# Two chunks of a gated feed-forward in seven-product form on 64x64 tiles

## The chip, the cores and the metric

The kernel runs on one core of a Trainium2 chip. The metric is the device time of one execution in microseconds, lower is better. TensorE (PE) does the matrix products, VectorE (DVE), ScalarE (ACT) and GpSimd (POOL) work on tiles, and SyncE (SP) issues most of the transfers. A tile in SBUF or PSUM has 128 rows (partitions); matrix products write to PSUM, which has eight banks of 512 float32 a row.

## The reference

An attention block (a sketch of degree two, four batches, four heads, 1088 positions, 32 per head) gives 4352 tokens of 128 features. They go through a gated feed-forward of width 1536, all in float32:

```python
gate = 1.0 / (1.0 + np.exp(-(x @ w_gate)))   # x: 4352 x 128, w_gate: 128 x 1536
val = x @ w_val                              # w_val: 128 x 1536
return (gate * val @ w_out).astype(np.float32)   # w_out: 1536 x 128
```

The change touches the feed-forward alone.

## The kernel before

The tokens are kept transposed, in `xT`, 128 features by 4352 tokens. They are cut into nine chunks: 0 to 7 of 512 tokens and a last one of 256. The width of 1536 is cut into twelve blocks j of 128. The unit of the loop is a wave (`w1`): for one j of one chunk PE makes gate and value, each 128x512, by four products of 128 rows, 64 columns and 512 tokens (L556), into two banks of a buffer `wave` that exists twice. Such a product gives two matmul records in the trace. ACT then makes the sigmoid `sg` from the gate half (L564), and DVE multiplies it with the value half into `g` (L599, L592 for the last chunk). One wave later the buffer's turn comes again, so the mult of wave n must be over before wave n+2 starts.

For chunks 1 to 7 the product with w_out is done by pairs of j. The two 64-column halves and the two 256-token halves of a pair make a 2x2 block product, and it is done in seven products in place of eight (L381, in `w2_a` and `w2_b`). POOL makes the four differences of tokens that it needs (`token_sums`, L371); the sums of weights, `ws`, are made once at the start. The results gather in two PSUM banks, `acc0` and `acc1`. At the end of a chunk ACT copies halves across (L487, L522, L529), DVE adds (L496) and transposes (L533), and SP issues the stores (L393): four where the chunk lies in one batch, eight where it lies in two (chunk 6 does, chunk 7 does not). The last chunk has six waves of two j each, and its w_out products have the tokens in the columns of the array (`w2_end`, L451).

The order of every engine's work is the order in which the program states it. Function `slot` runs one wave after the other: the mult of the wave before, the w_out products that are due, then the new wave. The attention work of batches 1 to 3 is put between the waves by hand, in `plan`. Waves are counted through: wave 0 is the first of chunk 0, waves 24 to 35 belong to chunk 2, wave 71 is the last of chunk 5, and chunks 6 and 7 are waves 72 to 95. The tokens of batch 3, from token 3264 on, are written to `xT` by DVE from 197.22 us on; chunk 6 begins at token 3072.

Of the kernel before, what the change touches and what calls it, by code (L numbers as in the profile page):

```python
# [8 lines left out]
F32 = mybir.dt.float32  # L9
# [3 lines left out]
ALU = mybir.AluOpType  # L13
ACTF = mybir.ActivationFunctionType
MUL = ALU.mult

P = 128


@with_exitstack  # L20
def kernel(
# [12 lines left out]
    nc = tc.nc  # L34
# [3 lines left out]
    F = R * R  # L38
# [3 lines left out]
    assert DM == H * D == P and D == 32 and R == 8 and S % 32 == 0 and NTOK % 512 == 256  # L42

    T = S // 32

    NJK = 9
    KBASE = [0, 9, 17, 25]
# [5 lines left out]
    ld = ctx.enter_context(tc.tile_pool(name="ld", bufs=1))  # L53
    sbA = ctx.enter_context(tc.tile_pool(name="sbA", bufs=2))
    raw = ctx.enter_context(tc.tile_pool(name="raw", bufs=NJ // 2))
    sbN = ctx.enter_context(tc.tile_pool(name="sbN", bufs=1))
    sbG = ctx.enter_context(tc.tile_pool(name="sbG", bufs=3))

    dram = ctx.enter_context(tc.tile_pool(name="dram", bufs=1, space=bass.MemoryType.DRAM))

    psm = ctx.enter_context(tc.tile_pool(name="psm", bufs=2, space=bass.MemoryType.PSUM))
    pso = ctx.enter_context(tc.tile_pool(name="pso", bufs=1, space=bass.MemoryType.PSUM))
    ps2 = ctx.enter_context(tc.tile_pool(name="ps2", bufs=1, space=bass.MemoryType.PSUM))

    ctx.enter_context(tc.manual_schedule(
            engines={
# [62 lines left out]
    class Short:  # L129
# [31 lines left out]
        def total(self):  # L161
            nc.gpsimd.tensor_tensor(  # L162
                out=self.head, in0=self.head, in1=self.tail.bitcast(I32), op=ALU.add
            )
# [183 lines left out]

    xT = const.tile([P, NTOK], F32, tag="xT")

    moe = {"sum": -1, "ci": 0, "w": 0, "n": 0, "ready": 0, "acc": None, "gate": None, "todo": [], "late": [], "copies": []}

    def fast(ci):
        return 0 < ci < len(tok_chk) - 1 and tok_chk[ci][1] == TCH

    def weight_sums(n0, n1):
        w = w_sb[:, 2].rearrange("p (n f) d -> p f n d", f=2)[:, :, n0:n1]
# [22 lines left out]
    def product(out, lhsT, rhs, start, stop):  # L380
        nc.tensor.matmul(  # L381
            out=out, lhsT=lhsT, rhs=rhs, start=start, stop=stop, skip_group_check=True
        )
# [18 lines left out]

    def store_end(acc):
        b, r = divmod(tok_chk[-1][0], S)
        o_sb = [sbA.tile([P, P], F32, tag="o_sb", name="o_end") for _ in range(2)]
        for u, copy in enumerate((nc.scalar.copy, nc.vector.tensor_copy)):
            copy(out=o_sb[u], in_=acc[u])
        for u, eng in enumerate((nc.scalar, nc.sync)):
            eng.dma_start(
                out=bass.AP(  # L410
                    tensor=out.tensor,
                    offset=out.offset + (b * S + r // 32 + u) * DM,
                    ap=[[T * DM, 32], [2 * DM, 4], [1, DM]],
                ),
                in_=o_sb[u],
            )

    def w2(ci, j0, jn, g):
# [13 lines left out]
        if j0 + jn == NJ:  # L432
# [2 lines left out]
            moe["store"] = lambda: store(  # L435
                ci, lambda g4: o_sb[32 * g4 : 32 * g4 + 32], nc.scalar
            )

    def w2_end(ci, j0, jn, g):
        if j0 == 0:  # L440
            moe["sum"] = ci
            moe["acc"] = [
                pso.tile([P, TCH], F32, tag="acc0", name="moeout0")[:, :DM],
                ps2.tile([P, 2, TCH], F32, tag="two", name="moeout1")[:, 0, :DM],
            ]
        acc = moe["acc"]
        for u in range(2):
            for jj in range(jn):
                j = j0 + jj
                for c in (u * P, u * P + 64):  # L450
                    nc.tensor.matmul(  # L451
                        out=acc[u][c % P : c % P + 64],
                        lhsT=g[:, jj, c : c + 64],
                        rhs=w_sb[:, 2, j, :],
                        start=(j == 0),
                        stop=(j == NJ - 1),
                    )
        if j0 + jn == NJ:
            store_end(acc)


    fst = {}

# [31 lines left out]
    def add(out, in0, in1):  # L495
        nc.vector.tensor_tensor(out=out, in0=in0, in1=in1, op=ALU.add)  # L496
# [44 lines left out]
    def w1():  # L541

        ci = moe["ci"]
        t0, tw = tok_chk[ci]
        jn = TCH // tw
        j0 = moe["w"] * jn
        wv = psm.tile([P, 2, TCH], F32, tag="wave", name="wave")

        tp = tw // 2 if ci == 0 and j0 == 0 else tw
        turn = (moe["w"] // 2) % 2  # L550
        for o in range(0, tw, tp):
            for which in range(2):
                for jj in range(jn):
                    for c in (0,) if ci == 0 else (1 - turn, turn):
                        d = slice(0, P) if ci == 0 else slice(64 * c, 64 * c + 64)
                        nc.tensor.matmul(  # L556
                            out=wv[d, which, jj * tw + o : jj * tw + o + tp],
                            lhsT=w_sb[:, which, j0 + jj, d],
                            rhs=xT[:, t0 + o : t0 + o + tp],
                            start=True,  # L560
                            stop=True,
                        )
        sg = sbG.tile([P, TCH], F32, tag="sg", name="sg")
        nc.scalar.activation(out=sg, in_=wv[:, 0], func=ACTF.Sigmoid)  # L564
        if ci == 0:
            if j0 == 0:
                step("final", 2)
                step("sign", 3, bank="acc1")
            if j0 == 1:
                step("final", 3)  # L570
            if 1 < j0 < NJ - 1:
                narrow_w(j0 + 1, 3)
            if j0 > 0:
                narrow_w(j0 + 2, 1)
                narrow_w(j0 + 2, 2)
            if j0 < 3:
                narrow_w(j0 + 3, 0)
            if j0 > 1:
                narrow_w(j0 + 4, 0)
            if j0 == NJ - 3:  # L580
                weight_sums(0, NJ // 4)
            if j0 == NJ - 1:
                weight_sums(NJ // 4, NJ // 2)
        if moe["w"] % 2 == 0:
            moe["g"] = sbG.tile([P, 2, TCH], F32, tag="g", name="g")
        pair, odd, n = moe["g"], moe["w"] % 2, moe["n"]

        def glu():
            g = pair[:, odd]
            todo = moe["todo"]  # L590
            if jn == 2:
                nc.vector.tensor_tensor(  # L592
                    out=g.rearrange("p (j u s y) -> p j y u s", j=2, u=2, y=4),
                    in0=wv[:, 1].rearrange("p (j y u s) -> p j y u s", j=2, u=2, y=4),
                    in1=sg.rearrange("p (j y u s) -> p j y u s", j=2, u=2, y=4),
                    op=MUL,
                )
            else:
                nc.vector.tensor_tensor(out=g, in0=wv[:, 1], in1=sg, op=MUL)  # L599
            if not fast(ci):  # L600
                lag = 4 if ci else 2
                part = (ci, j0, jn, g.rearrange("p (j t) -> p j t", j=jn))
                todo.append((n + lag, lambda: (w2_end if ci else w2)(*part)))
                return
            if not odd:
                moe["t"] = raw.tile([P, 4, HALF], F32, tag="w_in", name="tsum")
            token_sums(pair, moe["t"], odd)
            if odd:
                part = (ci, j0 // 2, pair, moe["t"])
                todo.append((n + 3, lambda: w2_a(*part)))  # L610
                todo.append((n + 4, lambda: w2_b(*part)))

        moe["gate"] = glu
        moe["w"] += 1
        moe["n"] += 1
        if j0 + jn == NJ:
            moe["ci"] += 1
            moe["w"] = 0

    def glu():  # L620
        if moe["gate"] is not None:
            moe["gate"]()
            moe["gate"] = None

    def slot(group, waves, behind=None):

        if group is not None:
            group()
        todo = moe["todo"]
        for _ in range(waves):  # L630
            more = moe["ci"] < len(tok_chk)
            if more and sum(tok_chk[moe["ci"]]) > moe["ready"]:
                break
            glu()
            for _ in range(2 if moe["ci"] >= len(tok_chk) - 1 else 1):
                if moe["late"]:
                    moe["late"].pop(0)()
            while todo and todo[0][0] <= moe["n"]:
                todo.pop(0)[1]()
            if behind is not None:  # L640
                behind()
                behind = None
            if more:
                w1()
            for copy in moe["copies"]:
                copy()
            moe["copies"] = []
            if more:
                continue
            if not todo:  # L650
                break
            else:
                todo.pop(0)[1]()

    kT_of, qT_of = {}, {}

# [688 lines left out]
    slot(None, 1)  # L1345
    slot(lambda: parts(1), 1)
    moe["store"]()

    def until(n):
        slot(None, n - moe["n"])  # L1350
# [3 lines left out]
    for b in range(2, B):  # L1354
# [24 lines left out]
        load_kq(b + 1)  # L1379
        until(next(at))  # L1380
        slot(lambda: parts(b), 1)
    slot(None, 10**3)


# [28 lines left out]
```

## Time and profile before

| | |
|---|---|
| median of 3 runs | 289.92 us (289.42 to 290.87) |
| span of the profiled execution | 288.1 us |
| what the median has beyond that span | 1.8 us |
| PE busy | 282.6 us, 98% of the span |
| DVE busy | 170.5 us, 59% |
| POOL busy | 160.0 us, 56% |
| ACT busy | 106.6 us, 37% |
| gate/value products of all waves (L556) | 820 records, 201.4 us |
| sigmoid (L564) | 102 x 597 ns |
| mult (L599) | 96 x 688 ns |
| differences of tokens on POOL (L371) | 168, 0.79 to 0.82 us each |
| last PE record ends | about 284.9 us |

In the profile's lines a group is named by its line, its engine and its operation, then the tile written, `<-`, the tiles read, the shape and the count; what follows is the start and the length in us, or for a group the busy time and the mean. "128*64 128x512" is a product with weights of 128 rows and 64 columns and a moving tile of 128 x 512. PEld is the loading of weights, SPq and ACTq are the transfers that SP and ACT issue. In a list of windows each engine has its busy time and its number of instructions, and then follow the granted clock of PE (1.00 is all of it), the busy share of the transfer engines and their GB/s. Ends of PE records are modelled, and the records of neighbouring products overlap, so that a step is best read from start to start.

### The profile page before, as it was taken

To read this page: it belongs to the slowest core of one execution; us is meant where nothing else is said; L and a number is where in the kernel's file an instruction comes from. 1 tells how busy PE (TensorE), PEld (TensorE's weight loads), DVE (VectorE), ACT (ScalarE), POOL (GpSimd) and SP (SyncE) were. 2 spreads that over 40 slices of the span, in tenths; PEclk is the share of its full clock that TensorE was granted. 3 is DMA by queue.
4 is the path that set the end of the run, shared out by engine and by line. 5 is a ranking of instruction groups with operands and counts; after the bars stand their busy time and mean duration, and the time that the engine had idled before them with its cause. 6 is when DMAs were issued, how large, how long until landed. Compare 5 with 4: busy or idle time off the path is not lost.

```text
span 288.1 us, 5783 instructions
## 1 busy us (share of the span) xinstructions
PE 282.6 (98%) x2260; PEld 135.1 (47%) x2260; DVE 170.5 (59%) x292; ACT 106.6 (37%) x215; POOL 160.0 (56%) x222
## 2 busy tenths in 40 slices
PE   8899999999999999999999999999999999999995
PEld 4454433354444444535444445444444444444685
DVE  6977788945748547668446485767245223522571
ACT  3688833222334322523244222532243224421341
POOL 2666682667466387383565496483564646555200
PEclk9999999999999999999999999999999999999999
DMA  7995441766500385352000683020001000020012
GB/s 220 348 360 124 104 156 43 171 150 157 164 3 2 77 198 166 92 161 32 1 0 12 162 158 123 2 30 9 0 3 23 14 2 0 4 35 1 0 19 40
DMA packets 28891, 24.24 MB, mean 84 GB/s; under 512 B 18560, under 2 KB 24064, under 8 KB 28864
## 3 DMA queue, kind: packets, MB, share of 16 engines
q1 hardware_dynamic: 25888, 22.10, 30.1%
q10 hardware_dynamic: 2976, 1.77, 2.1%
q8 instruction: 18, 0.29, 0.4%
q14 instruction: 9, 0.07, 0.1%
HBM read 20.60 MB, written 3.26 MB: 83 GB/s over the span
## 4 chain that ended last, share of the span: by engine, by line
PE 97%; ACT 1%; POOL 0%; DVE 0%; issue 0%
PE wave L556 61%; PE prod L381 22%; PE moeout L425 4%; PE moeout L451 2%; PE warm L301 2%; PE kvz L912 1%; PE nps L1270 1%; PE kps L693 1%; PE kvz L899 1%; PE cqps L839 1%; PE nps L1102 0%; PE denj L1041 0%; PE nps L1054 0%; PE dps L1083 0%; ACT asb L810 0%; POOL gh L727 0%
## 5 line engine op out<-in xcount | busy, mean ns | idle before, releaser
L556 PE MATMUL wave<-xT,w_sb 128*64 128x512 f32 (+3 forms) x820 | 201.4, 565 | 0.1
L564 ACT ACTIVATE sg<-wave 128x512 f32<-128x512 f32 x102 | 60.9, 597 | 158.3 <-PE wave L556 152.3
L599 DVE TENSOR_TENSOR g<-wave,sg 128x512 f32<-128x512 f32 x96 | 66.1, 688 | 87.9 <-ACT sg L564 86.3
L371 POOL TENSOR_TENSOR tsum<-g,tsum 128x256 f32<-128x256 f32 x84 | 68.6, 817 | 71.0 <-DVE g L599 70.9
L556 PEld LDWEIGHTS wave<-xT,w_sb 128*64 128x64 f32 (+1 forms) x820 | 71.0, 140 | 72.7 <-issue 53.0
L371 POOL TENSOR_TENSOR tsum<-g 128x256 f32<-128x256 f32 x84 | 66.6, 793 | 22.1 <-DVE g L599 21.5
L381 PE MATMUL prod<-tsum,ws 128*64 128x256 f32 x252 | 68.4, 380 | 0.0
L381 PE MATMUL prod<-g,w_sb 128*64 128x256 f32 (+1 forms) x170 | 50.3, 378 | 0.0
L381 PEld LDWEIGHTS prod<-tsum,ws 128*64 128x64 f32 x252 | 34.0, 137 | 13.1 <-issue 9.7
L381 PEld LDWEIGHTS prod<-g,w_sb 128*64 128x64 f32 x170 | 23.0, 137 | 30.1 <-issue 25.8
L381 PE MATMUL prod<-tsum,w_sb 128*64 128x256 f32 x84 | 25.0, 380 | 0.0
L381 PE MATMUL prod<-g,ws 128*64 128x256 f32 x84 | 25.0, 379 | 0.0
L162 POOL TENSOR_TENSOR head<-head,tail 128x384 int32<-128x384 int32 (+1 forms) x13 | 13.2, 1023 | 4.4 <-DVE head L157 4.4
L381 PEld LDWEIGHTS prod<-g,ws 128*64 128x64 f32 x84 | 11.5, 137 | 5.7
L425 PE MATMUL moeout<-g,w_sb 128*128 128x512 f32 (+1 forms) x26 | 12.4, 596 | 0.0
L381 PEld LDWEIGHTS prod<-tsum,w_sb 128*64 128x64 f32 x84 | 11.3, 137 | 1.3 <-issue 1.0
L592 DVE TENSOR_TENSOR g<-wave,sg 128x512 f32<-128x512 f32 x6 | 6.8, 1134 | 6.3 <-ACT sg L564 4.7
L772 DVE TENSOR_TENSOR kp<-kab 128x1152 f32<-128x1152 f32 (+1 forms) x8 | 10.2, 1289 | 0.0
L892 DVE TENSOR_TENSOR qp<-qp,bq 128x1152 f32<-128x1152 f32 (+1 forms) x7 | 10.1, 1444 | 0.0
L496 DVE TENSOR_TENSOR res<-prod,other 128x256 f32<-128x256 f32 x14 | 5.9, 425 | 6.3 <-ACT other L487 4.8
L141 POOL TENSOR_SCALAR head<-cap 128x384 f32<-128x384 f32 (+1 forms) x13 | 6.2, 483 | 4.6 <-ACT cap L140 4.6
L152 ACT ACTIVATE tail<-w_in,two__157 128x384 f32<-128x384 uint32 (+1 forms) x12 | 7.3, 618 | 0.0
(130 smaller groups left out, 197.5 us busy)
## 6 DMA issues: line engine op xcount, KB each, us to landing
qp<-dq SPq DMA_DIRECT2D x7, 576.0 KB
bq<-dq SPq DMA_DIRECT2D x14, 288.0 KB
kq<-in_k_dram SPq DMA_DIRECT2D x3, 544.0 KB
kq<-in_q_dram SPq DMA_DIRECT2D x3, 544.0 KB
w_in<-in_moe_w_out_dram SPq DMA_DIRECT2D x6, 256.0 KB
w_in<-in_moe_w_gate_dram SPq DMA_DIRECT2D x5, 256.0 KB
w_in<-in_moe_w_val_dram SPq DMA_DIRECT2D x5, 256.0 KB
v<-in_v_dram SPq DMA_DIRECT2D x8, 144.0 KB
```

Source lines behind the costliest of these rows:

```text
L141: nc.gpsimd.tensor_scalar(out=self.head.bitcast(F32), in0=self.cap, scalar1=122880.0, scalar2=2.0**-15, op0=ALU.min, op1=ALU.max,)
L152: nc.scalar.activation(out=self.tail, in_=self.lo, func=ACTF.Identity, bias=two, scale=2.0**-51)
L162: nc.gpsimd.tensor_tensor(out=self.head, in0=self.head, in1=self.tail.bitcast(I32), op=ALU.add)
L371: nc.gpsimd.tensor_tensor(out=t[:, u], in0=in0, in1=in1, op=ALU.subtract)
L381: nc.tensor.matmul(out=out, lhsT=lhsT, rhs=rhs, start=start, stop=stop, skip_group_check=True)
L425: nc.tensor.matmul(out=moe["acc"][d], lhsT=w_sb[:, 2, j, d], rhs=g[:, jj], start=(j == 0), stop=(j == NJ - 1),)
L556: nc.tensor.matmul(out=wv[d, which, jj * tw + o : jj * tw + o + tp], lhsT=w_sb[:, which, j0 + jj, d], rhs=xT[:, t0 + o : t0 + o + tp], sta ...
L564: nc.scalar.activation(out=sg, in_=wv[:, 0], func=ACTF.Sigmoid)
L592: nc.vector.tensor_tensor(out=g.rearrange("p (j u s y) -> p j y u s", j=2, u=2, y=4), in0=wv[:, 1].rearrange("p (j y u s) -> p j y u s", j ...
L599: nc.vector.tensor_tensor(out=g, in0=wv[:, 1], in1=sg, op=MUL)
L772: eng.tensor_tensor(out=KP[b][:, pi, j0:j1].rearrange("p j m (i l) -> p (j m) i l", i=R), in0=bass.AP(tensor=a0.tensor, offset=a0.offset, ...
L892: nc.vector.tensor_tensor(out=q0, in0=q0, in1=half(BQ[b], n), op=MUL)
```

## The change

Chunks 6 and 7 get their gate and value in another form, in a section of its own at the end of the program. The 2x2 block product here is that of the upper and the lower 64 features with the gate and the value weights of a block, on one side, and with the two token halves, on the other. Seven products (P1 to P7) replace eight. Each is on one half of the rows: 64 features, 256 tokens, and, for one j, two halves of 64 columns. For a pair of j this makes 14 items (the second j is marked by a prime, `P1'`), each of two products of 64x64x256. Items on the lower and the upper half of the rows are listed in turns, and they write to different banks.

The whole section is written out item by item in a string, `ORDER`, that gives each engine its sequence. The letter says what the item is and the number after the colon the pair (0 to 5 are chunk 6, 6 to 11 chunk 7, -2 and -1 the last two pairs of chunk 5, whose w_out is held back into the section):

- P: a gate/value product on half the rows. P1 and P2 go into bank GA, P5 and P3 into GC, P6, P7 and P4 into V; each bank exists twice, so that six banks take the place of the two `wave` buffers and of the bank pair `two`.
- Aa, Ac, Sa, Sc on ACT: copy GA to V, copy GC to SBUF, and the two sigmoids, once GA and GC are complete.
- D1, D2 on DVE: V plus the copy, into GC and into SBUF; M1, M2: the two halves of the mult. Q0 to Q3 on POOL: the differences of tokens for w_out.
- W: two w_out products, on the lower (WL), the upper (WU) or all rows (WF), A or B naming the accumulator.
- E, F: a chunk's end. ACT copies an accumulator to SBUF, SP copies halves across the rows (two transfers for A, three for B), DVE adds (F0 to F5), and F6 transposes and starts the stores on SP.
- C, Y, Z, O: the last chunk's gate/value products, sigmoid, mult and w_out products, now listed between the ends of chunks 6 and 7. T: a sum of tokens of `xT` on POOL.

The seven products need sums of the gate and value weights. For these ACT issues seven transfers (64 rows x 3 x 256 columns, across the halves). They are listed for waves 21 to 24, but stated only once wave 23 is, so that six stand in a row behind wave 23's sigmoid and one behind wave 24's. DVE makes ten sums, one each behind a mult from wave 24 to wave 61, two of 128x768 and eight of 64x768. They need also four differences of tokens of each chunk on POOL, of which chunk 6's are put among the last four waves of chunk 5, and copies of the tokens across the rows, issued by SP.

```diff
+ORDER = """
+P5:1 P1:0 T0:1 P1':1 WLA:-2.1 P1:1 P1':0 P5':1 P5':0 Aa:0 WUB:-2.0 P5:0 WLA:-2.0 Aa:1 P6':0 P2':0
+P6:0 Ac:0 P6':1 P2:1 Ac:1 P6:1 D1:0 P2':1 P2:0 D1:1 Sa:1 P7':0 P3':0 P7:0 P3:0 Sa:0 P3':1 P7':1 D2:0
+Sc:0 WUB:-1.0 WLA:-1.0 P3:1 WLA:-1.1 M2:0 WUB:-1.1 P7:1 Sc:1 P4':0 P5':2 Q0:0 D2:1 P4:0 P1:2 P5':3
+P1':2 M1:0 P1':3 P4':1 WUA:-2.0 M2:1 P4:1 Aa:2 Q1:0 P1:3 P5:2 P5:3 P2:2 M1:1 Q0:1 Ac:2 P6':2
...
+Q1:10 C1:1 C2:1 Y:1 Q2:11 C3:1 F1:0 C1:2 Q3:8 Z:1 C0:2 C2:2 Q3:9 Y:2 C3:2 F2:0 C0:3 Q3:11 Z:2 C1:3
+C2:3 Q2:10 Y:3 C3:3 F3:0 WFA:9.1 Q3:10 Z:3 WFA:11.1 WFA:9.0 WFA:8.1 F4:0 WFA:11.0 F5:0 WFA:10.0
+WFA:8.0 F6:0 WFA:10.1 WFB:9.0 EA:1 WFB:9.1 WFB:10.0 WFB:11.1 WFB:11.0 WFB:8.0 C0:4 EB:1 C1:4 F0:1
+C2:4 Y:4 C3:4 F1:1 O0:0 O0:1 Z:4 C1:5 O3:3 O2:0 O2:1 C0:5 F2:1 O0:4 O3:4 Y:5 F3:1 O3:1 O2:4 F4:1
+C3:5 F5:1 O3:2 O1:0 O2:3 C2:5 F6:1 O1:4 O1:2 Z:5 O1:3 O0:3 O3:0 O0:2 O1:1 O2:2 O2:5 O1:5 O0:5 O3:5
+"""
...
+    SECT, HELD, BUF = 6, 2, 0
+    LOAD_AT, SUM_AT = (21, 21, 22, 22, 23, 23, 24), (25, 30, 32, 34, 37, 45, 46, 49, 55, 61)
...
     dram = ctx.enter_context(tc.tile_pool(name="dram", bufs=1, space=bass.MemoryType.DRAM))
 
-    psm = ctx.enter_context(tc.tile_pool(name="psm", bufs=2, space=bass.MemoryType.PSUM))
     pso = ctx.enter_context(tc.tile_pool(name="pso", bufs=1, space=bass.MemoryType.PSUM))
-    ps2 = ctx.enter_context(tc.tile_pool(name="ps2", bufs=1, space=bass.MemoryType.PSUM))
+    early = ctx.enter_context(ExitStack())
+    psm = early.enter_context(tc.tile_pool(name="psm", bufs=2, space=bass.MemoryType.PSUM))
+    ps2 = early.enter_context(tc.tile_pool(name="ps2", bufs=1, space=bass.MemoryType.PSUM))
 
...
+    fw = []
+
+    def cross_weights():
+        sbw.close()
+        fwp = ctx.enter_context(tc.tile_pool(name="fwp", bufs=1))
+        fw.append(fwp.tile([P, 3, NJ, P], F32, tag="fw", name="fw"))
+        gate, val = (w_sb[:, k].rearrange("p (n f) d -> p n (f d)", f=4) for k in range(2))
+        slots = [fw[0][:, k].rearrange("p (n f) d -> p n (f d)", f=4) for k in range(3)]
+        loads, sums = [], []
+        for turn in range(2):
+            lead, tail = halves(turn)
+            cols = slice(2 * P * turn, 2 * P * turn + 2 * P)
+            g, v = gate[:, :, cols], val[:, :, cols]
+            f = [x[:, :, cols] for x in slots]
+            for dst, src in ((lead, tail), (tail, lead)):
+                if turn == 0 or dst == lead:
+                    loads.append((f[0][dst], g[src]))
+                loads.append((f[2][dst], v[src]))
+            every = slice(0, P)
+            ops = [
+                (every, f[1], v, f[2], ALU.add),
+                (lead, f[2], g, f[0], ALU.add),
+                (lead, f[2], f[2], f[1], ALU.subtract),
+            ]
+            if turn == 0:
+                ops += [(tail, f[2], f[0], f[2], ALU.subtract), (tail, f[0], f[1], f[0], ALU.subtract)]
+            else:
+                ops += [(tail, f[0], f[1], g, ALU.subtract), (tail, f[1], g, v, ALU.subtract)]
+            sums += [
+                lambda o=o: nc.vector.tensor_tensor(
+                    out=o[1][o[0]], in0=o[2][o[0]], in1=o[3][o[0]], op=o[4]
+                )
+                for o in ops
+            ]
+        loads = [lambda o=o, i=i: nc.scalar.dma_start(out=o, in_=i) for o, i in loads]
+        for at, many in ((LOAD_AT, loads), (SUM_AT, sums)):
+            for n in at:
+                moe["prep"].append((n, many.pop(0)))
+            assert not many
+        moe["prep"].sort(key=lambda x: x[0])
...
+                if ci == SECT - 1 and j0 // 2 >= NJ // 2 - HELD:
+                    moe["held"].append(part[2:])
+                    return
...
+            while moe["prep"] and moe["prep"][0][0] < moe["n"]:
+                moe["prep"].pop(0)[1]()
...
     moe["store"]()
+    cross_weights()
...
-    slot(None, 10**3)
+    YT = {}
+
+    def load_y(c):
+        t = sbA.tile([P, 2 * H * W1], F32, tag="qp", name="yt")
+        y = t[:, : 2 * TCH].rearrange("p (k t) -> p k t", k=2)
+        s = t[:, 2 * TCH : 4 * TCH].rearrange("p (u t) -> p u t", u=4)
+        YT[c] = y, s
+        t0 = tok_chk[SECT + c][0]
+        for k, src in enumerate((LO, HI)):
+            for dst in (LO, HI):
+                nc.sync.dma_start(out=y[dst, k], in_=xT[src, t0 : t0 + TCH])
+
+    def x_sum(c, u):
+        y, s = YT[c]
+        out, in0, in1 = (
+            (s[:, 0], y[:, 0, HALF:], y[:, 0, :HALF]),
+            (s[:, 1], y[:, 1, HALF:], s[:, 0]),
+            (s[:, 2], y[:, 1, HALF:], y[:, 0, HALF:]),
+            (s[:, 3], y[:, 1, :HALF], s[:, 1]),
+        )[u]
+        nc.gpsimd.tensor_tensor(out=out, in0=in0, in1=in1, op=ALU.subtract)
+
+    def section():
...
+        early.close()
+        pg = ctx.enter_context(tc.tile_pool(name="pg", bufs=1, space=bass.MemoryType.PSUM))
+        bank = [pg.tile([P, TCH], F32, tag=f"b{x}", name=f"b{x}") for x in range(6)]
+        GA, GC, V = (bank[4], bank[BUF]), (bank[5], bank[BUF + 1]), (bank[2 - BUF], bank[3 - BUF])
...
+        def feature(k, nn, w):
+            lead, tail = halves(w)
+            j = 2 * (w % per) + nn
+            f, gate, val = fw[0][:, :, j], w_sb[:, 0, j], w_sb[:, 1, j]
+            y, s = YT[w // per]
+            even = w % 2 == 0
+            rows, lhsT, rhs, dst = {
+                "P1": (lead, gate if even else f[:, 0], y[:, 0, :HALF], GA),
+                "P2": (lead, f[:, 0] if even else gate, y[:, 1, :HALF], GA),
+                "P5": (lead, f[:, 1], s[:, 0], GC),
+                "P3": (lead, f[:, 2], y[:, 1, HALF:], GC),
+                "P6": (tail, f[:, 0], s[:, 1], V),
+                "P7": (tail, f[:, 2 if even else 1], s[:, 2], V),
+                "P4": (tail, val if even else f[:, 2], s[:, 3], V),
+            }[k]
+            start = k in ("P1", "P5") and (k, w) not in started
+            for c in range(2):
+                product(
+                    dst[w % 2][half_of(c), nn * HALF : (nn + 1) * HALF],
+                    lhsT[rows, half_of(c)], rhs[rows], start, False,
+                )
+
...
+        def gated(k, w):
+            ga, gc, v = GA[w % 2], GC[w % 2], V[w % 2]
+            s5, sg, c2, g = s5s[w % 2], sgs[w % 3], c2s[w % 3], gs[w % len(gs)]
+            two = lambda x: x.rearrange("p (j t) -> p j t", j=2)
+            first, second = slice(0, HALF), slice(HALF, TCH)
+            if k == "Aa":
+                nc.scalar.copy(out=v, in_=ga)
+            elif k == "Ac":
+                nc.scalar.copy(out=s5, in_=gc)
+            elif k == "Sa":
+                nc.scalar.activation(out=sg[:, :, first], in_=two(ga), func=ACTF.Sigmoid)
+            elif k == "Sc":
+                nc.scalar.activation(out=sg[:, :, second], in_=two(gc), func=ACTF.Sigmoid)
+            elif k == "D1":
+                add(gc, v, s5)
+            elif k == "D2":
+                add(c2, v, s5)
+            elif k == "M1":
+                nc.vector.tensor_tensor(out=g[:, :, first], in0=two(v), in1=sg[:, :, first], op=MUL)
+            else:
+                nc.vector.tensor_tensor(out=g[:, :, second], in0=two(c2), in1=sg[:, :, second], op=MUL)
+
...
+            e, x1, x2, x5, r0, y = ev[c]
+            e = e[:, 0 if b == "A" else 1]
+            nc.scalar.copy(out=e, in_=acc[b, c])
+            if b == "A":
+                nc.sync.dma_start(out=x1[LO], in_=e[HI, :HALF])
+                nc.sync.dma_start(out=x1[HI], in_=e[LO, :HALF])
+            else:
+                nc.sync.dma_start(out=x2[LO], in_=e[HI, HALF:])
+                for rows in (LO, HI):
+                    nc.sync.dma_start(out=x5[rows], in_=e[LO, HALF:])
+
...
+            o_sb = sbA.tile([P, TCH // 32, 32], F32, tag="o_sb", name="o_sb")
+            nc.vector.transpose(out=o_sb.rearrange("p t x -> p (t x)"), in_=y)
+            store(SECT + c, lambda g4: o_sb[32 * g4 : 32 * g4 + 32])
...
+                if "end" not in acc:
+                    acc["end"] = [pso.tile([P, TCH], F32, tag="acc0", name="moeout0")[:, :DM], V[0][:, :DM]]
...
+    at = NJ * SECT
+    until(at - 6)
+    load_y(0)
+    for u in range(4):
+        until(at - 4 + u)
+        x_sum(0, u)
+    until(at)
+    glu()
+    if SECT + 1 < len(tok_chk) - 1:
+        load_y(1)
+    for x in moe["late"]:
+        x()
+    section()
 
 
 # ---- launch: one core; inputs and outputs as the reference has them ----
```

## The prediction

> **What bounds the kernel now.** I read the page first: busy times, the slices, the chain by engine.
>
> ```profile
> span 288.1 us, 5783 instructions
> ...
> PE 282.6 (98%) x2260; PEld 135.1 (47%) x2260; DVE 170.5 (59%) x292; ACT 106.6 (37%) x215; POOL 160.0 (56%) x222
> ...
> PE   8899999999999999999999999999999999999995
> ...
> PEclk9999999999999999999999999999999999999999
> ...
> PE 97%; ACT 1%; POOL 0%; DVE 0%; issue 0%
> ```
>
> PE is the bound from end to end at full granted clock; every other engine is idle for 40% or more. So a PE step saved is a step gained, as long as PE goes on without a gap. Then the windows, where the columns are PE, PEld, DVE, ACT, POOL, granted clock:
>
> ```profile
> 200.00:220.00 20.00, 20.00 (x124) 8.92 (x122) 7.75 (x14) 7.14 (x15) 12.43 (x19) 1.00 0.00 1
> 220.00:240.00 20.00, 20.00 (x124) 9.05 (x122) 6.43 (x10) 4.78 (x8) 11.69 (x17) 1.00 0.09 14
> ```
>
> PE has no gap in the very stretch that the change rewrites. So each wait that the new order brings is paid in full. The chain of waits gives the price of a step:
>
> ```profile
> 268.41 0.86 PE prod L381 x8
> 269.27 1.73 PE wave L556 x16
> ...
> 281.33 3.56 PE moeout L451 x63
> ...
> 284.91 0.29 DVE o_end L407
> ```
>
> Eight records of w_out products (128x64, 256 columns, two records a product, the two column halves side by side) take 0.86 us: a step of two products is 0.43 us. A wave is 1.72 (8 records, 512 columns); the line of 1.73 shows x16 because another step's records overlap. Last, the timeline, at the places that the change touches and at rows like its new work:
>
> ```profile
> 72.11 1.06 PE L1270 MATMUL nps<-qp,nd 64*32 64x512 f32 x16
> ```
> ```profile
> 187.67 1.84 POOL L371 TENSOR_TENSOR tsum<-g 128x256 f32<-128x256 f32 x1
> ...
> 206.96 0.60 ACT L564 ACTIVATE sg<-wave 128x512 f32<-128x512 f32 x1 [1.97 <-PE wave L556]
> ...
> 207.59 0.69 DVE L599 TENSOR_TENSOR g<-wave,sg 128x512 f32<-128x512 f32 x1 [1.81 <-ACT sg L564]
> ...
> 190.17 3.78 SPq L393 DMA_DIRECT2D out_dram<-o_sb  x8
> ```
>
> The first is the only work on half the rows: sixteen records, eight tiles at a time, begin in two rounds 0.43 us apart and are done in 1.06. The second is POOL while DVE works from SBUF to SBUF (0.73 otherwise). The next two are the last handoff ahead of the new section; the last is SP issuing a chunk's eight stores.
>
> **The change part by part.** The profiled execution has a span of 288.1; the runs' median is 289.92, so 1.8 us lie around the span, and I carry them over. I sum against 288.1.
>
> 1. Gate/value of chunks 6 and 7: removed are 24 waves x 1.72 = 41.3 us. Added are 12 pairs x 14 items (each two 64x64 products on one half of the rows). An item of the lower and one of the upper half make a step of 0.43, if they run side by side: 84 x 0.43 = 36.1. Gain 5.2 us (12 x 0.43). The w_out of 14 pairs keeps its cost: 70 half items in 35 steps and 14 full ones, 49 x 0.43, as the 14 x 3.5 full steps before. In the order each upper item has a lower neighbour that writes another bank.
>
> 2. Is a step of eight records still 0.43? Row for: the sixteen records at 72.11, 6.7 ns from issue to issue, two rounds. Row for the density: L451's 63 records with as many weight loads in 3.56 us, so 16 instructions in 0.45 us, where a step needs 16 in 0.43. Bounds: 0 to 0.02 a step (0.45 less 0.43), 119 steps: 0 to 2.4 us. I take 0, since L451's 16 rounds of 0.215 and an end of 0.16 give 3.6 by themselves.
>
> The Trainium skill ("TensorE: Matmul & The Clock Gate", Part 3, "Measured speedup vs the span model") speaks against it: four row tiles gave 3.07 times one, not four. By that a step would be 0.56 and the section some 15 us longer; the sixteen records at 72.11 do not agree, they lose nothing to 0.43 a round.
>
> The same page ("Wait — 56ns, not 53.3ns?") has a matmul cost about 62 ns of sequencer time where hardware decoding is off: eight of them are 0.50 us a step, some 8 us in all. The 6.7 ns between issues at 72.11 say that it does not bind here.
>
> 3. Start of the section: its first product goes into the bank of wave 71, so it waits for that wave's mult. Before, PE ended wave 71 at 206.76 and went on in the other buffer; the mult ended at 208.28. Now PE waits from about 206.75 to 208.33: 1.6 us (1.5 to 1.7).
>
> 4. Handoffs inside the section. A pair's P7 may run when DVE's D1 has read the V bank, and D1 waits for two ACT copies. For the first pair, counted from the section's first matmul: its P1' is in the third step and ends at 1.46 (3 x 0.43 and 0.17, by which a record outlasts its step); ACT then makes Aa:0, Aa:1 and Ac:0 in a row, 0.6 each (nearest row: L810, 128x512 out of PSUM, 589 ns), to 3.35; D1 takes 0.69 (L599's shape), to 4.1. Eighteen items, nine steps, stand ahead of P7' in the order: PE wants it at 3.87, and waits 0.3. Later pairs have five steps (2.15) between P6 and P7 for one D1 of 0.7 to 1.0, so nothing in the sum; but PE takes its items in order, an upper item waits with a late lower one, and 24 more such handoffs (two a pair) follow. I take 0.6, bounds 0.1 to 1.7 (24 x 0.07, a D1 that starts behind another in one case of ten).
>
> 5. The end: chunk 6's eight stores go on SP after its transpose, 3.78 us, and SP also issues the five copies across halves of chunk 7. Call T the end of WFA. Stores begin at T-0.4; the copies are issued by T+3.5, and land 1.5 later with two more issues ahead: T+5.3. Behind them on DVE: F0:1 and F1:1 (0.43 each, L496) and Z:4 (1.13, L592): T+7.4. PE wants O0:4 after 6 steps of WFB, 4 of C, and four O's and half steps: T+6.2. Wait 1.2 to 1.3; bounds 0.6 (issues at 0.4) to 2.1 (0.6).
>
> 6. Preparing weight sums in chunks 2 to 5. ACT issues seven DMAs, six of them in a row behind a sigmoid: 6 x 0.47 (row: four in 2.01 at 76.32) = 2.85. The sigmoid of wave 24 slips from 81.05 to 82.35, its mult to 83.7, and wave 26 needs the buffer at 84.27: hidden. The first sum waits for its fourth load and holds the next mult to about 86.1 against 86.4: hidden, barely. The ten sums (934 ns for 768 elements, 0.69 for 512) are some 9 us of DVE, one between two mults each; a period of a pair is 5 us with 1.4 of mults: hidden. I take 0.3, bounds 0 to 1.9 (one wait of 0.5 and one sum too late by 1.4).
>
> 7. POOL: the four differences of chunk 6's xT ahead of the section delay the token sums of a pair by 0.75 at a slack of 1.1: 0.1 (0 to 0.5). In the section four sums a pair (0.73 to 0.82) fill 3.3 of each 4.5 us, hidden. SP's loads of xT's halves wait for xT's part at 197.2 and land by 199.2, well ahead of 208.
>
> 8. Changes from whole to half rows and back, twice: 0.2 (0 to 0.5), from the 0.17 that a record's end takes.
>
> Sum: -5.2 +0 +1.6 +0.6 +1.3 +0.3 +0.1 +0.2 = -1.1. Span 287.0, time 288.8 to 288.9. Low ends: -5.2 +1.5 +0.1 +0.6 = -3.0 (286.9). High ends: -5.2 +2.4 +1.7 +1.7 +2.1 +1.9 +0.5 +0.5 = +5.6 (295.5).
>
> **The rivals.** A measurement tells about 0.5% from no change: 1.45 us.
>
> A, the forecast: the gain mostly eaten by the start and the end, 288.0 to 290.0.
>
> B: the waits come at their cheap ends, and the dense order holds: only the start's 1.6 and 0.6 at the end are left, 5.2-2.2-0.4 = 2.6 less at best, 287.3 to 288.2. For it: DVE, ACT and POOL have 40% free, and the handoffs of the middle have twice what they need. Against: PE's order is fixed, so each late handoff is paid.
>
> C, on the other side: the steps on half rows are longer. Place: the 119 steps. Each 9 ns over 0.43 costs 1.1 us, so from 0.439 the gain is gone, and from 0.451 (2.5 us) it is slower by over 0.5%. Price: at L451's whole 3.82 us for 64 records (16 instructions in 0.478) it is 119 x 0.048 = 5.7, so 294.6; at its 3.56, 0.015 a step or 1.8, so 290.7. I put it at 290.7 to 294.6. For it: no row holds eight 64x64 tiles that accumulate. Against: the sixteen records at 72.11.
>
> D: ACT's row of DMA issues and the sums do hold up PE in chunks 2 to 5 (1.9, point 6's high end), or POOL's sums stretch as at 187.67 (1.84 instead of 0.73) when M2 works from SBUF to SBUF. One such stretch is 1.1, and with two or three of the twelve M2 on the path it is 2.2 to 3.3: 290.5 to 292.2. Against: POOL at 3.3 of 4.5 has room for one stretch a pair.
>
> **How the numbers follow.** A 0.38, B 0.30, C 0.20, D 0.12. The time is A's, 288.9. Faster by over 0.5% is under 288.47: all of B and a fifth of A, 0.37. Slower is over 291.37: three quarters of C, 0.15, and half of D, 0.06, and 0.02 for several of A's high ends at once: 0.23. Within 0.5%: the rest, 0.40. The range from B's 287.3 to 291.9 leaves out 0.04 below and, above, some 0.12 of C and 0.04 of D. A's own range is 288.0 to 290.0.
>
> **What would show it.** Step 1 and 2: in the windows of the section, 20 us hold 46 steps; a PE row of the products on half rows with pairs that start within 20 ns of each other and steps 0.43 apart. Step 3: a gap of 1.6 at the section's start, named after the mult of wave 71. Step 4: PE idle behind DVE's first add under 0.5. Step 5: a gap of 1.3 near the end, behind the mult Z, and SP's stores in front of its copies. Step 6: no PE idle between 79 and 150. The prediction is wrong if the steps are not 0.43, if PE waits again and again in the section (over 0.1 a pair), or if the end's copies wait for more than SP.

## The result, and the profile after

The changed kernel took 293.42 us (median, 292.39 to 294.32) against 290.39 us for the kernel before (the three runs known ahead and a fourth of 292.33): 1.0% longer, ratio 1.010 with an interval of 1.0065 to 1.0135. The medians of the kernel before beside the experiments, 289.88 and 290.03, are lower, and against them the loss is 3.4 to 3.5. The forecast was 288.9, and the range ended at 291.9.

The page of the changed kernel, in the order in which that of before was read:

```profile
span 290.3 us, 7144 instructions
...
PE 279.6 (96%) x2880; PEld 153.5 (53%) x2880; DVE 199.6 (69%) x329; ACT 114.8 (40%) x224; POOL 175.5 (60%) x230
...
PE   8899999999999999999999999999899999999955
...
PE 88%; DVE 4%; DMA 2%; SPq 2%; ACT 1%; issue 1%; POOL 1%; ACTq 0%; DVEq 0%
```

PE has less work than before (279.6 for 282.6 busy) in a longer span (290.3 for 288.1). One slice more is an 8 (from 203 to 210 us), and the last two are 5, where before only the last was. The chain is now 12% other engines, where it was 3%. PE's waits, longest first (total, times, longest), say where:

```profile
PE moeout L463 <- DVE g L1619: 2.9, 1, 2.9
PE b L463 <- DVE g L650: 1.4, 1, 1.4
...
PE wave L615 <- DVE g L650: 0.7, 1, 0.7
```

The first is at the end, behind the mult Z:4. The second is at the section's start, and the third in chunk 2, where the weight sums are prepared. In the section itself the windows have no gap:

```profile
220.00:240.00 20.00, 20.00 (x374) 14.85 (x368) 15.34 (x22) 12.45 (x24) 17.92 (x24) 1.00 0.08 19
240.00:260.00 20.00, 20.00 (x376) 19.48 (x372) 14.37 (x23) 9.56 (x19) 11.33 (x16) 1.00 0.14 28
```

There are 374 records in 20 us where there were 124, and PE is busy throughout. From the section's first record (209.91) to the last chunk's first (261.88) it took 51.97; 119 steps of 0.4315, the common distance from start to start, are 51.35.

Against the kernel before, the profiled execution's time goes as follows. Delays up to wave 71 are differences of the starts of the same wave's sigmoid.

| part | forecast | measured |
|---|---|---|
| steps saved | -5.2 | -5.2 (12 x 0.4315) |
| steps longer, handoffs | 0 + 0.6 | 0.6 |
| weight sums prepared (waves 23 to 27) | 0.3 | 0.9 |
| differences on POOL (waves 69 to 70) | 0.1 | 0.5 |
| wait at the section's start | 1.6 | 1.6 |
| wait at the end | 1.3 | 3.1 |
| changes of mode | 0.2 | in the 0.6 above, about 0.1 |
| before the first wave; after the last product | 0 | 0.1; 0.2 |
| sum | -1.1 | +1.8 |

The spans differ by 2.2, so 0.4 is left unassigned. The change back to whole rows is the distance from the last start on half rows, 261.57, to the next product, 261.88: 0.31, where half a step is 0.216. The wait at the end is counted from 278.55, where the steps before it are over, to 281.64; the record in front of it ends later. The end itself, on SP, DVE and PE:

```profile
271.90 5.07 SPq L475 DMA_DIRECT2D out_dram<-o_sb  x8
277.06 0.47 SPq L1580 DMA_DIRECT2D xb<-e  x1
...
279.73 0.42 DVE L555 TENSOR_TENSOR r<-e,xb 128x256 f32<-128x256 f32 x1 [7.86 <-DMA xb<-e]
...
280.54 1.05 DVE L1619 TENSOR_TENSOR g<-b,sg 128x512 f32<-128x512 f32 x1
...
281.64 0.44 PE L463 MATMUL moeout<-w_sb,g 128*64 128x128 f32 x4 [2.91 <-DVE g L1619]
```

The mechanism is the one forecast: eight stores, then the copies, then two adds, then Z:4. Two pieces are longer. The eight stores took 5.07 and not 3.78: seven of them took 0.32 to 0.46, as forecast, and one took 1.76. And the first add started 2.2 after the issue of the second copy began, where 1.5 had been taken for the landing. The one long store is no accident of this profile: in the five other profiled runs with the eight stores in front one store took 1.48 to 2.07.

In the one run of four where PE kept its full clock the span was 290.3; in the other three the mean granted clock was 0.994 and the span 291.3 to 292.3. The kernel before stood at 0.998 or more in all 41 runs beside the experiments. So the median's 3.0 is more than the profile's 2.2, and the experiments look for that as well.

### The profile page after: what moved, and what is told of

It is laid out like the page before. It is cut to its first block, busy times and chain, and to the rows that moved or that the text cites. A ratio compares the mean times of both kernels' runs of the same rounds, so it can differ in the third digit from the quotient of the medians.

```text
span 290.3 us, 7144 instructions
## 1 busy us (share of the span) xinstructions
PE 279.6 (96%) x2880; PEld 153.5 (53%) x2880; DVE 199.6 (69%) x329; ACT 114.8 (40%) x224; POOL 175.5 (60%) x230
## 4 chain that ended last, share of the span: by engine, by line
PE 88%; DVE 4%; DMA 2%; SPq 2%; ACT 1%; issue 1%; POOL 1%; ACTq 0%; DVEq 0%
PE wave L615 41%; PE prod L463 19%; PE b L463 16%; PE moeout L507 4%; PE warm L337 2%; SPq L475 2%; PE kvz L960 1%; DVE g L1619 1%; DMA fw<-w_sb 1%; PE kps L741 1%; PE nps L1318 1%; PE moeout L463 1%; DMA xb<-e 1%; DVE g L650 1%; PE kvz L947 1%
## 5 line engine op out<-in xcount | busy, mean ns | idle before, releaser
L615 PE MATMUL wave<-xT,w_sb 128*64 128x512 f32 (+2 forms) x532 | 142.2, 590 | 0.8 <-DVE g L650 0.7
L650 DVE TENSOR_TENSOR g<-wave,sg 128x512 f32<-128x512 f32 x72 | 49.5, 687 | 43.2 <-ACT sg L623 42.4
L463 PE MATMUL prod<-tsum,ws 128*64 128x256 f32 (+1 forms) x312 | 78.3, 379 | 0.0
L463 PE MATMUL prod<-g,w_sb 128*64 128x256 f32 (+2 forms) x210 | 52.3, 377 | 0.0
L463 PE MATMUL b<-yt,fw 64*64 64x256 f32 x528 | 46.6, 377 | 1.4 <-DVE g L650 1.4
L463 PEld LDWEIGHTS prod<-tsum,ws 128*64 128x64 f32 (+1 forms) x312 | 40.3, 135 | 9.5 <-issue 5.4
L463 PEld LDWEIGHTS prod<-g,w_sb 128*64 128x64 f32 (+1 forms) x210 | 24.6, 135 | 20.8 <-issue 16.1
L463 PEld LDWEIGHTS b<-yt,fw 64*64 64x64 f32 x528 | 29.4, 133 | 7.2 <-DVE g L650 2.3
L463 PE MATMUL prod<-tsum,w_sb 128*64 128x256 f32 (+1 forms) x104 | 30.3, 378 | 0.0
L463 PE MATMUL prod<-g,ws 128*64 128x256 f32 (+1 forms) x104 | 30.2, 378 | 0.0
## 6 DMA issues: line engine op xcount, KB each, us to landing
bq<-dq SPq DMA_DIRECT2D x14, 288.0 KB
```

The source lines that it names most:

```text
L463: nc.tensor.matmul(out=out, lhsT=lhsT, rhs=rhs, start=start, stop=stop, skip_group_check=True)
L615: nc.tensor.matmul(out=wv[d, which, jj * tw + o : jj * tw + o + tp], lhsT=w_sb[:, which, j0 + jj, d], rhs=xT[:, t0 + o : t0 + o + tp], sta ...
```

## The experiments

My theory was that four waits of PE ate the gain, each from a queue of another engine, and that the half-row steps cost what they should. The rivals were that the waits only move, or that the dense section itself costs the time.

**The start.** The wave buffers were given back in one piece, so the section's first product waited for the last mult, although its bank had been wave 70's (by the order in which the program hands out the banks). The pools are split and closed one mult apart:

```diff
...
     until(at)
+    early.close()
+    pg = ctx.enter_context(tc.tile_pool(name="pg", bufs=1, space=bass.MemoryType.PSUM))
+    bank = [pg.tile([P, TCH], F32, tag=f"b{x}", name=f"b{x}") for x in range(4)]
     glu()
+    last_wave.close()
+    pv = ctx.enter_context(tc.tile_pool(name="pv", bufs=1, space=bass.MemoryType.PSUM, side="right"))
+    bank += [pv.tile([P, TCH], F32, tag=f"b{x}", name=f"b{x}") for x in (4, 5)]
...
+        GA, GC, V = (bank[2], bank[0]), (bank[3], bank[1]), (bank[4], bank[5])
```

> The changed kernel, with the last wave's two PSUM banks in a pool of their own and the other four given back one mult earlier, so that the section's first product waits for the mult of wave 70 and no longer for that of wave 71. Theory (the start's wait is paid in full by PE, and its bank was free all along): PE goes on at about 208.35 instead of 209.91, 1.5 us faster than the changed kernel (span 288.7 to 288.9). Rival (the wait only moves: the first ACT copies go into wave 71's banks and hold up P6): 0 to 0.5 faster, with a PE wait behind ACT's copy.

The changed kernel, and below it this run (PE's first product of the section and DVE's mult of wave 71 in each):

```profile
209.16 0.69 DVE L650 TENSOR_TENSOR g<-wave,sg 128x512 f32<-128x512 f32 x1 [1.82 <-ACT sg L623]
209.91 0.43 PE L463 MATMUL b<-yt,fw 64*64 64x256 f32 x2 [1.41 <-DVE g L650]
```
```profile
208.13 0.43 PE L474 MATMUL b<-yt,fw 64*64 64x256 f32 x2
208.86 0.69 DVE L661 TENSOR_TENSOR g<-wave,sg 128x512 f32<-128x512 f32 x1 [1.82 <-ACT sg L634]
```

The section began at 208.13, ahead of wave 71's mult; the wait of 1.4 is gone and none took its place. (This run's first wave came 0.3 earlier, so 1.5 of the 1.8 is the wait.) At full clock the spans were 288.0 to 288.6, 1.7 to 2.3 below 290.3. But the median was 292.27, because five of eight runs had a clock of 0.988 or 0.994, the profiled one among them. Its windows at the end (PE's busy time is the second figure, its granted clock the third from the end):

```profile
278.00:280.00 2.00, 0.18 (x2) 0.18 (x4) 1.97 (x4) 0.00 (x0) 0.00 (x0) 0.77 0.28 68
280.00:282.00 2.00, 2.00 (x18) 1.82 (x20) 1.90 (x5) 0.00 (x0) 0.00 (x0) 0.50 0.00 0
282.00:284.00 2.00, 2.00 (x18) 1.75 (x16) 0.00 (x0) 0.00 (x0) 0.00 (x0) 0.50 0.44 66
284.00:286.00 2.00, 2.00 (x20) 1.67 (x18) 1.07 (x1) 0.00 (x0) 0.00 (x0) 0.52 0.46 69
286.00:288.00 2.00, 2.00 (x38) 1.77 (x34) 0.01 (x1) 0.15 (x1) 0.00 (x0) 1.00 0.00 0
```

PE idles for 2.9 behind Z:4, and the clock is 0.50 for over six microseconds: 18 to 20 records in 2 us instead of 38. That looks like a second price of the same wait; a run further down tests it.

**The stores at the end.** Chunk 6's stores are stated after chunk 7's copies:

```diff
-            store(SECT + c, lambda g4: o_sb[32 * g4 : 32 * g4 + 32])
+            put = lambda: store(SECT + c, lambda g4: o_sb[32 * g4 : 32 * g4 + 32])
+            moe["put"] = put if c == 0 else put()
...
                     nc.sync.dma_start(out=x5[rows], in_=e[LO, HALF:])
+                if c == 1:
+                    moe["put"]()
```

> The changed kernel, with chunk 6's eight stores stated after chunk 7's five copies across halves, so that SP issues the copies first. Theory (the stores stand in front of the copies, and DVE's Z:4 stands behind the adds that wait for them): the PE wait of 2.9 behind Z near the end is gone, 2.8 to 3.1 us faster than the changed kernel, span 287.2 to 287.5. Rival (the copies' own way, or DVE's adds, are as long): under 1 us faster, and a wait behind Z of over 2 stays.

Median 289.77 of ten runs (nine from 289.50 to 290.05, one of 294.24 at full clock), ratio to before 0.999 (0.997 to 1.001), span 287.7: the whole loss is gone. But the stores did not all move. SP's queue here was ordered by the planner, the step that lays out the instructions, and not by the program's text. It left four stores ahead of the copies, and two between them:

```profile
271.34 1.77 SPq L475 DMA_DIRECT2D out_dram<-o_sb  x4
273.20 0.47 SPq L1580 DMA_DIRECT2D xb<-e  x1
273.71 1.89 SPq L1581 DMA_DIRECT2D xb<-e  x1
275.65 1.12 SPq L475 DMA_DIRECT2D out_dram<-o_sb  x2
```

```profile
PE moeout L463 <- DVE g L1622: 0.9, 1, 0.9
```

So the wait fell from 2.9 to 0.9, where the theory had it gone; the issue of the second copy took 1.89 here, 0.59 in the changed kernel. From the last chunk's first product to PE's end it is 22.96 for 24.99, 2.0 less. Against before, the median went from 3.0 above to 0.1 below: more than those 2.0. The clock was at 0.999 or more in every run, and this profiled run's first wave came 0.6 earlier than the changed kernel's.

**The order on DVE.** The stores stay in front, and the adds go behind the mult:

```diff
...
-C0:4 EB:1 C1:4 F0:1
-C2:4 Y:4 C3:4 F1:1 O0:0 O0:1 Z:4 C1:5
+C0:4 EB:1 C1:4
+C2:4 Y:4 C3:4 O0:0 O0:1 Z:4 F0:1 F1:1 C1:5
...
```

> The changed kernel, with chunk 7's adds F0 and F1 put behind the mult Z:4 in the order; SP's stores stay in front of the copies. Theory (the order on DVE turns SP's queue into a PE wait): no PE wait before Z:4's products, but Z:5 now ends at 284.0 and its products wait 1.3; 1.5 to 2 us faster than the changed kernel. Rival (SP's queue binds by itself through chunk 7's own stores): no faster by more than 0.5.

Median 290.17, ratio to before 1.000 (0.998 to 1.002); PE's last stretch 23.0, again 2.0 less. The one wait left at the end is 0.9 behind Z:5 (1.3 expected). SP's eight stores took 4.94 and the adds started only at 279.21, but Z:4 had started at 276.52:

```profile
276.52 1.11 DVE L1619 TENSOR_TENSOR g<-b,sg 128x512 f32<-128x512 f32 x1 [5.02 <-PE b L463]
```
```profile
PE b L463 <- DVE g L1619: 0.9, 1, 0.9
```

Moving two small adds did as much as moving the stores: the queue on SP cost PE time here only through what stood behind it on DVE.

**The second price.** Three products that nobody reads fill the wait:

```diff
-... F2:1 O0:4 ...
+... F2:1 X:0 O0:4 ...
...
+            elif k == "X":
+                for _ in range(3):
+                    product(V[1], w_sb[:, 2, 0, :], xT[:, :TCH], True, True)
```

> The changed kernel, with three products of 128x128x512 put on PE into the wait of 2.9 us near the end; they write to a free bank and nothing reads it. Theory (the wait has a second price: PE idle for 3 us lets the granted clock fall to 0.50 for 3 to 7 us in part of the runs): the same work ends at the same time as in the runs at full clock, the clock of every run is 0.998 or more, median 292.2 to 292.6 with few above 293. Rival (the spread comes from elsewhere): runs at 0.988 to 0.994 as before, median over 293.

Four runs, all at 0.998 to 1.000, 291.93 to 292.53, median 292.13: 2.1 above the 290.03 of the kernel before beside it, where the changed kernel had been 3.0 above its own. The filled stretch, and the product that had waited:

```profile
278.36 3.37 PE L463 MATMUL b<-xT,w_sb 128*64 128x256 f32 x10
281.69 0.44 PE L463 MATMUL moeout<-w_sb,g 128*64 128x128 f32 x4
```

The waiting product starts at 281.69, where it was 281.64, so the wait's first price (3.1) stays; only the slow clock goes. That makes about 0.9 of the median the clock's (3.0 less 2.1; the changed kernel's one run at full clock, 292.39, is 1.0 below its median).

**The weight transfers.** SP issues them instead of ACT:

```diff
-        loads = [lambda o=o, i=i: nc.scalar.dma_start(out=o, in_=i) for o, i in loads]
+        loads = [lambda o=o, i=i: nc.sync.dma_start(out=o, in_=i) for o, i in loads]
```

> The changed kernel, with the seven weight transfers issued by SP instead of ACT. Theory (ACT's sigmoid of wave 24 waits behind six issues of 0.77 us and holds up the mults): PE's 0.9 us around 84 to 85 is gone or down to 0.3 (the first sum on DVE may still wait for its fourth transfer): 0.6 to 0.9 faster. Rival (the landing of the transfers and the sums on DVE are what holds the mult): 0 to 0.2 faster, and PE's wait at 85 stays behind the mult.

Median 293.17 with most runs at a low clock, so the sigmoids tell more. From wave 24 on no time is lost any more. But the planner put the transfers on SP at 42 to 47, ahead of batch 1's other transfers, which came 1.9 later; an attention product on DVE (L940) then came late, and waves 22 and 23 lost 0.5. The gain up to wave 71 is 0.4, outside both expectations. The issues took 0.61 to 0.95 on SP too (0.62 to 0.95 on ACT): these transfers are dear to issue on either engine.

**The preparation alone**, in the kernel before:

```diff
     moe["store"]()
+    cross_weights()
...
+            while moe["prep"] and moe["prep"][0][0] < moe["n"]:
+                moe["prep"].pop(0)[1]()
```

> The kernel before, with only the seven weight transfers on ACT and the ten sums on DVE added; their results are not used. Theory (six issues of 0.77 us stand in front of wave 24's sigmoid, and the sums are hidden): 0.9 us slower than before (0.8 to 1.1), all of it between the sigmoids of waves 23 and 27. Rival 1 (the sums cost too, later): over 1.3 slower, sigmoids later by more and more up to wave 62. Rival 2 (what was seen there belongs to the section): 0 to 0.3 slower.

Median 290.69 against 290.03, ratio 1.003 (1.0007 to 1.0053), so 0.7 longer. In the profile 0.9 is lost between the sigmoids of waves 23 and 27, and nothing after; the sums are hidden, the row of issues is not. ACT's lines in that kernel:

```profile
78.47 4.59 ACTq L397 DMA_DIRECT2D fw<-w_sb  x6
83.17 0.60 ACT L612 ACTIVATE sg<-wave 128x512 f32<-128x512 f32 x1 [4.15 <-DMA fw<-w_sb]
```

Six issues took 4.6, and wave 24's sigmoid started at 83.17, 2.6 late by the sigmoid of wave 23.

**The differences of tokens**, on DVE instead of POOL:

```diff
...
-        until(at - 4 + u)
-        x_sum(0, u)
+        until(at - 2 + u // 2)
+        x_sum(0, u, nc.vector)
```

> The changed kernel, with the four differences of chunk 6's tokens on DVE ahead of the mults of waves 69 and 70, instead of on POOL from wave 68 on. Theory (POOL stood idle 5 us behind the copies of the tokens and the token sums of the last pairs came late by 0.5): the sigmoid of wave 70 is no later than that of wave 69, 0.5 us faster at the section's start. Rival (POOL is late without them, or DVE's extra work holds the mult as much): 0 to 0.1, wave 70 still 0.5 later.

Wave 70 is no later than wave 69 (0.54 each against the kernel before; it had been 1.06 and 1.57), as the theory has it. The median, 292.74, says little, since four of six runs had a clock of 0.994. POOL's lines in the changed kernel, and below them the kernel before:

```profile
201.40 0.73 POOL L1451 TENSOR_TENSOR yt<-yt 128x256 f32<-128x256 f32 x1 [5.19 <-DMA yt<-xT]
202.08 0.73 POOL L453 TENSOR_TENSOR tsum<-g,tsum 128x256 f32<-128x256 f32 x1
```
```profile
199.51 0.73 POOL L371 TENSOR_TENSOR tsum<-g,tsum 128x256 f32<-128x256 f32 x1 [4.35 <-DVE g L599]
```

POOL stood idle for 5.2 us until the copies of the tokens had landed, with the token sums of chunk 5 queued behind the difference. Most of this idle time, 4.4, is there before too. What counts is the sum behind it: it starts at 202.08 for 199.51, 2.6 later, of which 1.05 is the delay that the run has at this point anyway. The other 1.5 is twice the 0.75 of the forecast, which had looked at the length of the operation and not at when its input lands.

**All four.** The pools and the differences as above; the transfers in pairs behind two sigmoids, and the first sum two waves later; at the end ACT issues the two copies for accumulator A, and half of chunk 6's stores after the last sigmoid:

```diff
-    LOAD_AT, SUM_AT = (21, 21, 22, 22, 23, 23, 24), (25, 30, 32, 34, 37, 45, 46, 49, 55, 61)
+    LOAD_AT, SUM_AT = (23, 23, 24, 24, 28, 29, 30), (27, 30, 32, 34, 37, 45, 46, 49, 55, 61)
...
+            if c == 0:
+                store(SECT, rows, part=0)
+                moe["put"] = lambda: store(SECT, rows, nc.scalar, part=1)
...
+                eng = nc.scalar if c == 1 else nc.sync
+                eng.dma_start(out=x1[LO], in_=e[HI, :HALF])
+                eng.dma_start(out=x1[HI], in_=e[LO, :HALF])
```

> The changed kernel with all four waits dealt with: the banks as in the pools run; chunk 6's differences on DVE; the weight transfers two behind wave 23's sigmoid, two behind wave 24's, then one a wave, and the first sum two waves later; at the end the two copies for accumulator A of chunk 7 on ACT and the second half of chunk 6's stores on ACT after the last sigmoid. Theory (the four waits add: 1.5, 0.5, 0.9 and 3.1, and the steps on half rows cost what they should): 5.5 to 6 us faster than the changed kernel's 290.3 span, 284.3 to 284.8, so 286.3 to 286.8 and 1% faster than before. Rival (freed waits come back as others, or the half rows lose time): 287.5 or more.

Median 286.04 (285.70 to 286.20), a little under the 286.3 to 286.8 expected: ratio to before 0.986 (0.9845 to 0.988), faster than both kernels. Its page:

```profile
span 283.9 us, 7142 instructions
...
PE 278.2 (98%) x2880; PEld 152.4 (54%) x2880; DVE 202.1 (71%) x333; ACT 115.0 (41%) x224; POOL 172.9 (61%) x226
...
PE   8899999999999999999999999999999999999995
...
PE 95%; DVE 1%; DMA 1%; ACT 1%; issue 0%; POOL 0%; SPq 0%; DVEq 0%
```

In PE's row the 8 in the middle is gone, and only the last slice is a 5, as before the change. The span is 6.4 below the changed kernel's, against 1.6 + 0.5 + 0.9 + 3.1 = 6.1 for the four waits; the first wave came 0.6 earlier in this run, so 5.8 lies behind it. The waits add within 0.3, and none came back.

## Why the prediction was wrong

**Right: steps 1, 2, 4 and the rival C's fate.** The steps on half rows cost 0.4315 each, so rival C's condition did not come about, and the section took 0.6 over that, as the sum had it. That the 0.6 came out is partly luck: the first pair's handoff cost 0.06 and not 0.3, another behind D1 at 223.10 cost 0.14, and about 0.1 is the change back to whole rows, which had a term of its own in step 8. Step 2 and rival C read the same row differently (3.56 us for 63 records as 0.02 a step and as 0.015), and the row at 72.11 is not the only work on half the rows of before; neither moved the sum. The Trainium skill's two warnings ("TensorE: Matmul & The Clock Gate", "Measured speedup vs the span model" and "Wait — 56ns, not 53.3ns?") would, by the prediction's estimate, have made the section some 15 and some 8 us longer; 374 records in 20 us, one in 53 ns, without a gap show neither here.

**Step 3: right in size, wrong in reason.** The wait was 1.6. But the bank was not wave 71's: it was wave 70's, and the first product waited because the pool with both buffers was given back in one piece. The run with split pools shows it.

**Step 5 is the term that decided.** It had the right chain and 1.3 for it, up to 2.1; it measured 3.1. Stores at 0.47 gave 3.78 for eight; they took 5.07, because one of them took 1.76. From the second copy's issue to the add it was 2.2, not 1.5. The 3.78 came from the row at 190.17, in which no store was held up; for the 1.5 the text names no row, and the one copy for accumulator A whose landing the changed kernel's profile has, at 222.71, took 1.9. The step also costed the wait by its length alone: the granted clock halved around it in 16 of the 25 runs of kernels that have the wait, and the median pays about 0.9 more. No row of before shows PE idle for 3 us once it is running, so this price was without a bound, and the text should have said so.

**Step 6** took 0.47 for an issue of ACT from stores (the row that it names, four in 2.01, gives 0.50). These transfers took 0.62 to 0.95, 4.64 for six: 0.9 lost instead of 0.3. The sums it feared are hidden. So rival D was right in its first half, the row of issues, though at half its 1.9; POOL's sums in the section did not stretch (0.81 and 0.79 us on average).

**Step 7** gave POOL's differences 0.1 for their length; they cost 0.5, since the first waited for its copies with chunk 5's sums behind it. The copies were to land 2.0 after their part of `xT` was there (197.2 to 199.2); it was 3.1 (198.28 to 201.40).

Summed with what the runs show, the four waits come to 6.1, not to the 3.3 in the forecast, against the 5.2 gained. The waits stood where the forecast had them, the one at the start for another reason; what turned the sign were the sizes of two queues, SP's at the end and ACT's in chunk 2, POOL's input, and the clock.

## What to carry to other kernels

Where one engine is busy all the time, the gain is the easy part of the sum; what decides is each queue at the seams, counted in order: what is issued ahead, how long an issue of that very transfer takes, when its data lands, and what stands behind it on the waiting engine. One cheap move, two adds put behind a mult, took 2.0 us of PE's wait away, and with it the low clock. A pool closed in one piece makes its next user wait for the last reader of all of it.

## What the runs showed of the hardware

**The clock falls around a short wait.** In the run with split pools, PE was idle from 276.95 to 279.82 and its granted clock was 0.50 from about 279.1 until nearly 286. In the profiled run with the weight transfers on SP, PE had gone on at 280.54 after 2.65 us of waiting, and the clock fell only at about 281.3, for 3.4 us:

```profile
280.00:282.00 2.00, 1.46 (x18) 1.33 (x20) 1.91 (x5) 0.00 (x0) 0.00 (x0) 0.82 0.01 2
282.00:284.00 2.00, 2.00 (x18) 1.76 (x16) 0.71 (x1) 0.00 (x0) 0.00 (x0) 0.50 0.17 25
284.00:286.00 2.00, 2.00 (x30) 1.62 (x29) 1.03 (x1) 0.00 (x0) 0.00 (x0) 0.82 0.72 106
```

The changed kernel's wait of 2.9 left the clock alone in one run of four. Over the four kernels that have this wait (changed, pools, weight transfers, differences) the mean clock was 0.988 to 0.994 in 16 of 25 runs. Of the 28 runs of the kernels without that wait, or with it filled (stores, order on DVE, fill, all four), none was below 0.996. One of the ten runs of the preparation alone was at 0.988 without such a wait; its reason is open. The Trainium skill ("TensorE: Matmul & The Clock Gate", "What's actually happening") describes a gate that passes half the pulses after an idle window of about 3.4 us, and says that this window runs free. The halving agrees with these windows, and a window that runs free would explain why some runs are hit and others not. But the waits that did it here were 2.65 to 3.2 us, shorter than the page's window, and the measurement decides.

**An issue that meets a load of instructions can be slow.** In ten traces, of 1161 transfers issued by SP and ACT after the first 60 us, 33 took over 1.05 us to issue, and each of the 33 had a 16 KB packet of the instruction queue (q8) between 0.54 us before its start and 0.20 after. Of the 60 issues with a packet so near, 27 were not slow (0.30 to 0.97), and of the other 1101 none took over 0.95. In the changed kernel the slow ones are the 1.76 among the stores at the end (packet 0.16 after its start), two of the copies across halves, and a load at 120.06. The section makes such packets more frequent: eight between 213 and 263, where before there were three. That the packet is the cause was not tried.
